# Opening the first feed-forward of a fused attention and SwiGLU kernel with interleaved groups, fillers in the first norm, and column-tiled sums of squares

## The chip, the cores and the metric

The kernel runs on one core of a Trainium2 chip. The metric is device time in microseconds (us); lower is better. A core has several engines that run side by side and meet at semaphores: TensorE (PE in the profile, with its weight loads as PEld), VectorE (DVE), ScalarE (ACT), GpSimd (POOL) and SyncE (SP), and DMA queues that move data between main memory and the on-chip memory. Matmuls write to PSUM, an accumulator memory of few buffers; ACT and DVE read it out.

## The reference

Eight batches of attention with a squared ReLU in place of the softmax, then a root-mean-square norm, then a SwiGLU feed-forward without biases:

```python
# q, k, v: (8 batches, 12 heads, 448 positions, 64)
scores = (1/8) * q @ k.T                       # per batch and head
attn   = maximum(scores, 0)**2 / 448
x      = attn @ v                              # to (3584 tokens, 768)
rms    = sqrt(mean(x*x, axis=-1) + 1e-6)
xn     = x / rms * rms_g
g      = xn @ w_gate                           # 768 -> 1536
out    = (g * sigmoid(g)) * (xn @ w_val) @ w_out   # 1536 -> 768
```

The norm stands between the two halves: no projection of a batch can start until all 768 features of the batch are known.

## The kernel before

One batch is 448 tokens, S. The features lie on the 128 partitions in 6 k tiles (KT), the 1536 hidden features in 12 blocks (FT). P is 128, D is 64. The program fixes the order on each engine itself: the feed-forward of batch b is the main list of units, the attention and the norm of batch b+1 are the side list, and `merge` lays the side units between the main ones by estimated cost. `head` and `tail` are the shares of the main list that stay free of side units at its start and at its end.

```python
def merge(main, side, head=0.0, tail=0.0):
    total = sum(c for c, _ in main)
    ...
    n = len(side)
    for c, f in main:
        while k < n and done >= total * (head + (1.0 - head - tail) * k / n):
            out.append(side[k][1])
            k += 1
        out.append(f)
        done += c
    out.extend(f for _, f in side[k:])
    return out
```

PSUM is shared out in three pools. All projections, output pieces, transposes, sums of squares and fillers take one of three buffers in turn:

```python
ps_s = ... tile_pool(name="ps_s", bufs=2, space=PSUM)   # scores
ps_a = ... tile_pool(name="ps_a", bufs=1, space=PSUM)   # attention times v
ps_m = ... tile_pool(name="ps_m", bufs=3, space=PSUM)   # all else
```

Fillers are matmuls on a tile of zeros whose result nobody reads:

```python
def keep_busy(n):
    ps = ps_m.tile([P, S], FP32, name="psB", tag="mm")
    for _ in range(n):
        nc.tensor.matmul(out=ps[:], lhsT=ones_bf[:], rhs=busy_bf[:], start=True, stop=True)
```

In the attention, a group of scores is four matmuls on the two row halves of the array, into both score buffers. ACT (or DVE) applies the ReLU out of PSUM, and the squares are put off to a later unit. `attend` multiplies by v, and the tile of the output and its square follow on ACT and DVE:

```python
def attend(b, j):
    psAV = ps_a.tile([P, S], FP32, name="psAV", tag="ps_a")
    ...                                    # 8 matmuls on column halves
    nc.scalar.mul(out=xT[:, j, :], in_=psAV[:], mul=inv_attn)
    pending.append(lambda: nc.vector.tensor_tensor(          # the square
        out=x2s[b][:, j, :], in0=xT[:, j, :], in1=xT[:, j, :], op=ALU.mult))
```

The norm sums the squares over the partitions with a matrix of ones, so that every partition gets the sum; ACT takes the root, DVE the reciprocal, and DVE scales the six tiles one after the other:

```python
def norm(b):
    psSS = ps_m.tile([P, S], FP32, name="psSS", tag="mm")
    for kt in range(KT):
        nc.tensor.matmul(out=psSS[:], lhsT=ones_bf[:], rhs=x2s[b][:, kt, :],
                         start=(kt == 0), stop=(kt == KT - 1))
    ...
    nc.scalar.activation(out=rstd[:], in_=psSS[:], func=ACT.Sqrt, ...)
    act_table(ACT.Silu)
    nc.vector.reciprocal(out=rstd[:], in_=rstd[:])
    for kt in range(KT):
        nc.vector.scalar_tensor_tensor(out=xn[:, kt, :], in0=xTs[b][:, kt, :],
            scalar=g_sb[:, kt : kt + 1], in1=rstd[:], op0=ALU.mult, op1=ALU.mult)
```

The feed-forward: for each of the 12 blocks a gate group and a value group of 12 matmuls (6 k tiles, two column halves of 64), each followed by its reader; then output pieces of 24 matmuls, 512 and 256 columns wide:

```python
def gate(b, fb):
    psG = project(wg_sb, b, fb, "psG")     # 12 matmuls on column halves
    nc.scalar.activation(out=s[:], in_=psG[:], func=ACT.Silu)
    ...
def value(b, fb):
    psV = project(wv_sb, b, fb, "psV")
    nc.vector.tensor_tensor(out=hTs[...][:, fb, o:o+S], in0=sil[b, fb][:], in1=psV[:], op=ALU.mult)

def ffn(b):
    for fb in range(FT):
        units.append((1.13, gate)); units.append((1.13, value))
    for t in ...:                          # 3 or 4 tiles of 128 tokens
        units.append((2.56, outproj 512)); units.append((1.28, outproj 256))
```

The whole runs as attention and norm of batch 0 alone, and then eight times a feed-forward merged with the next attention and norm:

```python
for fn in merge([], attention(0) + [(1.1, lambda: norm(0))]): fn()
...
for b in range(B):
    side = attention(b + 1) + [(1.1, norm(b + 1))]
    main = ffn(b)
    ...
    for fn in merge(main, side, 0.3 if b == 0 else 0.0, 0.15): fn()
```

Of the kernel before, what the change touches and what calls it, by code (L numbers as in the profile page):

```python
# [8 lines left out]
FP32 = mybir.dt.float32  # L9
# [8 lines left out]
def merge(main, side, head=0.0, tail=0.0):  # L18


    total = sum(c for c, _ in main)
    if not main:
        return [f for _, f in side]
    out, done, k = [], 0.0, 0
# [9 lines that stand above are left out]
# [3 lines left out]
def kernel(  # L37
# [11 lines left out]
    nc = tc.nc  # L49
    P = nc.NUM_PARTITIONS  # L50
    B, H, S, D = q.shape
    T, DM = out.shape
    _, F = moe_w_gate.shape
    assert (T, DM) == (B * S, H * D) and 2 * D == P and S % NCH == 0 and B % 2 == 0
    PC = S // NCH
    KT, FT, HP = DM // P, F // P, H // 2
# [19 lines left out]
    ps_m = ctx.enter_context(tc.tile_pool(name="ps_m", bufs=3, space=bass.MemoryType.PSUM))  # L76
# [8 lines left out]
    def load(nm, b, h0=0, h1=H):  # L85
        runs = nm == "v" or b < PE_T
        if (nm, b) not in ld:
            shape = [PC, H, NCH * D] if runs else [PC, NCH, H * D]
            ld[nm, b] = ldpool.tile(shape, BF16, name=nm + "b", tag=nm + "b")
        t = ld[nm, b]  # L90
        src = src_of[nm][b, h0:h1]
        if runs:
            nc.gpsimd.dma_start(out=t[:, h0:h1, :], in_=src.rearrange("h (p c) d -> p h (c d)", c=NCH))  # L93
        else:
            nc.gpsimd.dma_start(  # L95
                out=t[:].rearrange("p c (h d) -> p c h d", d=D)[:, :, h0:h1, :],
                in_=src.rearrange("h (p c) d -> p c h d", c=NCH),
            )
# [4 lines left out]
    def transpose_dma(b):  # L103
        new_qkT(b)
        for ti, nm in enumerate(("k", "q")):
            for c in range(NCH):
                nc.sync.dma_start_transpose(
                    out=qkT[b][:, :, ti, c * PC : (c + 1) * PC], in_=ld[nm, b][:, c, :]
                )

    wg_sb = wpool.tile([P, KT, F], BF16, name="wg_sb", tag="wg")
    wv_sb = wpool.tile([P, KT, F], BF16, name="wv_sb", tag="wv")
# [18 lines left out]
    ones_bf = const.tile([P, P], BF16, name="ones_bf", tag="ones_bf")  # L131
# [4 lines left out]
# [4 lines that stand above are left out]
# [9 lines left out]
    def act_table(func):  # L149
        nc.scalar.activation(out=scrap[:], in_=eps_col[:], func=func)  # L150
# [73 lines left out]
    x2s = {}  # L224
# [23 lines left out]
    def attention(b):  # L248
        units = []

        def add(cost, *fns):
            units.append((cost, lambda: [f() for f in fns]))

        if b < PE_T:
            add(0.4, lambda: transposes(b, 0))
        for j in range(HP):
            add(0.5, lambda j=j: scores(b, j, (0, 1)))
            if b < PE_T and j + 1 < HP:
                add(0.4, lambda j=j: transposes(b, j + 1))
            if b == 0:  # L260
                add(0.3, lambda: keep_busy(2))
            add(1.2, lambda j=j: scores(b, j, (2, 3)), lambda j=j: j and attend(b, j - 1))
            if b == 0:
                add(0.3, lambda: keep_busy(2))
        add(0.1, flush)
        add(0.8, lambda: attend(b, HP - 1), flush)
        return units


    xns, hTs = {}, {}  # L270

    def norm(b):
        psSS = ps_m.tile([P, S], FP32, name="psSS", tag="mm")
        for kt in range(KT):
            nc.tensor.matmul(  # L275
                out=psSS[:], lhsT=ones_bf[:], rhs=x2s[b][:, kt, :],
                start=(kt == 0), stop=(kt == KT - 1),
            )
        rstd = npool.tile([P, S], FP32, name="rstd", tag="rstd", bufs=1)
        nc.scalar.activation(  # L280
            out=rstd[:], in_=psSS[:], func=ACT.Sqrt, scale=1.0 / float(DM), bias=eps_col[:]
        )
        act_table(ACT.Silu)
        nc.vector.reciprocal(out=rstd[:], in_=rstd[:])  # L284
        xn = npool.tile([P, KT, S], BF16, name="xn", tag="xn")
        for kt in range(KT):
            nc.vector.scalar_tensor_tensor(  # L287
                out=xn[:, kt, :], in0=xTs[b][:, kt, :], scalar=g_sb[:, kt : kt + 1], in1=rstd[:],
                op0=ALU.mult, op1=ALU.mult,
            )  # L290
        xns[b] = xn
        if b % 2 == 0:
            hTs[b // 2] = hpool.tile([P, FT, 2 * S], BF16, name="hT", tag="hT")

    def project(w_sb, b, fb, nm):
        ps = ps_m.tile([P, S], FP32, name=nm, tag="mm")
        for kt in range(KT):
            for h in range(0, P, D):
                nc.tensor.matmul(  # L299
                    out=ps[h : h + D, :], lhsT=w_sb[:, kt, fb * P + h : fb * P + h + D],  # L300
                    rhs=xns[b][:, kt, :], start=(kt == 0), stop=(kt == KT - 1),
                )
        return ps

    sil = {}

    def gate(b, fb):
        psG = project(wg_sb, b, fb, "psG")
        s = spool.tile([P, S], BF16, name="sil", tag="sil")
        nc.scalar.activation(out=s[:], in_=psG[:], func=ACT.Silu)  # L310
        sil[b, fb] = s

    def value(b, fb):
        psV = project(wv_sb, b, fb, "psV")
        o = (b % 2) * S
        nc.vector.tensor_tensor(  # L316
            out=hTs[b // 2][:, fb, o : o + S], in0=sil[b, fb][:], in1=psV[:], op=ALU.mult
        )

    osts = {}  # L320

    def outproj(i, t, o, w):
        ps = ps_m.tile([P, 512], FP32, name="psO", tag="mm")
        for fk in range(FT):
            for h in range(0, P, D):
                nc.tensor.matmul(  # L326
                    out=ps[h : h + D, :w], lhsT=hTs[i][:, fk, t * P + h : t * P + h + D],
                    rhs=wo_sb[:, fk, o : o + w], start=(fk == 0), stop=(fk == FT - 1),
                )
        if o == 0:  # L330
            osts[i, t] = opool.tile([P, DM], FP32, name="ost", tag="ost")
        ost = osts[i, t]
        nc.scalar.copy(out=ost[:, o : o + w], in_=ps[:, :w])  # L333
        if o + w == DM:
            g, end = t * P, (t + 1) * P
            while g < end:
                n = min(end, (g // PC + 1) * PC) - g
                b, c, p0 = 2 * i + g // S, g % S // PC, g % PC
                rows = out[b * S : (b + 1) * S, :].rearrange("(p u) m -> p u m", u=NCH)
                nc.sync.dma_start(  # L340
                    out=rows[p0 : p0 + n, c, :], in_=ost[g - t * P : g - t * P + n, :]
                )
                g += n

    def ffn(b):
        units = []
        for fb in range(FT):
            units.append((1.13, lambda fb=fb: gate(b, fb)))
            units.append((1.13, lambda fb=fb: value(b, fb)))
        full = S // P  # L350
        for t in range(full) if b % 2 == 0 else range(full, NT):
            units.append((2.56, lambda t=t: outproj(b // 2, t, 0, 512)))
            units.append((1.28, lambda t=t: outproj(b // 2, t, 512, DM - 512)))
        return units

    keep_busy(16)
    for fn in merge([], attention(0) + [(1.1, lambda: norm(0))]):
        fn()
    for nm in ("q", "k", "v"):
        load(nm, 1)  # L360
    load_wo(0, 2)
    load_wo(1, 2)
    for b in range(B):
        side = []
        if b + 1 < B:
            side = attention(b + 1) + [(1.1, lambda b=b: norm(b + 1))]
        main = ffn(b)
        if b + 2 < B:
            for nm in ("q", "k", "v"):
                load(nm, b + 2)  # L370
            at = len(main) * 2 // 3
            main[at:at] = [(0, lambda b=b: transpose_dma(b + 2))]
        for fn in merge(main, side, 0.3 if b == 0 else 0.0, 0.15):
            fn()


# [28 lines left out]
```

## Time and profile before

| what | value |
|---|---|
| time, median of 3 runs | 475.36 us (475.14 to 478.07) |
| span of the profiled run | 473.7 us |
| TensorE clock granted, mean over the span | 0.991 of full speed |
| PE busy | 455.2 us, 4696 matmuls |
| DVE busy | 283.5 us |
| ACT busy | 254.1 us |
| GpSimd busy | 55.7 us |
| sums of squares (psSS) | 48 matmuls of 128 x 128 by 448, 8 norms |
| reciprocal in each norm | 2953 ns on DVE |
| one scaling of a tile (xn) | 681 ns on DVE, 48 of them |

The names in the profile are those of the program: psG and psV are the gate and value groups, psO the output pieces, psS the scores, psAV the attention times v, psT the transposes, psSS the sums of squares, psB the fillers. "128\*64" behind a matmul is the part of the array that it uses, rows by columns: 128\*128 is the whole, 128\*64 one column half, 64\*128 one row half. L299 is a line of the kernel. A matmul's length in the timeline runs from its start to the end of its pipeline, and matmuls overlap, so what a group costs is read from the start of one group to the start of the next.

### The profile page before, as it was taken

Reading aid. Unit: us, or ns where it says so; the run is one execution under the profiler, and the core shown is the slowest. Engines: PE = TensorE matmul, PEld = TensorE weight load, DVE = VectorE, ACT = ScalarE, POOL = GpSimd, SP = SyncE. Lnnn points to the kernel's source line nnn. Section 1 sums busy time; section 2 is a strip of 40 time slices with the busy share of each in tenths; the row PEclk is TensorE's granted clock in tenths of the full one; section 3 lists DMA queues with packets and bytes.
Section 4 is the critical chain, followed back from the end, with each engine's and each line's share of the span. In section 5 each row is a group of like instructions: output and inputs, shape, how many; then the busy total and the mean of one; then the engine's idle time right before and its main releaser. Section 6 shows DMA issues by size and latency. Waiting matters only on the chain.

```text
span 473.7 us, 10771 instructions
## 1 busy us (share of the span) xinstructions
PE 455.2 (96%) x4696; PEld 246.7 (52%) x4696; DVE 283.5 (60%) x449; ACT 254.1 (54%) x380; POOL 55.7 (12%) x48
## 2 busy tenths in 40 slices
PE   7877999899999999999999999999999999999995
PEld 2323654454556544564546554564546644566563
DVE  2875389467773676567673767657663776752210
ACT  3871366466555566556564566465654566452221
POOL 8463000430004000130004000000000000000000
PEclk9997999999999999999999999999999999999999
DMA  9999999999906990099204990077002200021013
GB/s 105 198 204 199 208 165 137 98 210 148 84 2 95 211 122 1 2 189 176 29 1 69 218 142 1 1 142 135 1 1 61 76 1 1 1 68 35 1 35 100
DMA packets 128046, 43.55 MB, mean 92 GB/s; under 512 B 100608, under 2 KB 124416, under 8 KB 128000
## 3 DMA queue, kind: packets, MB, share of 16 engines
q0 software_dynamic: 88944, 23.60, 51.5%
q1 hardware_dynamic: 39056, 19.28, 21.3%
q8 instruction: 36, 0.59, 0.5%
q14 instruction: 10, 0.08, 0.1%
HBM read 47.19 MB, written 11.01 MB: 123 GB/s over the span
## 4 chain that ended last, share of the span: by engine, by line
PE 89%; DVE 5%; ACT 2%; DMA 1%; issue 1%; POOL 0%; DVEq 0%; ACTq 0%; POOLq 0%
PE psG L299 24%; PE psV L299 24%; PE psO L326 22%; PE psS L201 9%; PE psAV L230 8%; PE psSS L275 2%; DVE r L218 2%; DVE rstd L284 1%; ACT r L215 1%; DMA kb<-in_k_dram 1%; DVE xn L287 1%; DVE r L213 1%; PE psT L174 1%; PE psB L139 0%; ACT rstd L280 0%
## 5 line engine op out<-in xcount | busy, mean ns | idle before, releaser
L215 ACT ACTIVATE r<-psS 112x896 bf16<-112x896 f32 x147 | 128.5, 915 | 49.9 <-PE psS L201 49.7
L299 PE MATMUL psG<-xn,wg_sb 128*64 128x448 bf16 x1152 | 129.5, 357 | 5.1 <-DVE xn L287 5.1
L299 PE MATMUL psV<-xn,wv_sb 128*64 128x448 bf16 x1152 | 126.7, 355 | 0.0
L316 DVE TENSOR_TENSOR hT<-sil,psV 128x448 bf16<-128x448 bf16 x96 | 59.6, 621 | 98.8 <-PE psV L299 97.8
L326 PE MATMUL psO<-wo_sb,hT 128*64 128x512 bf16 (+1 forms) x1344 | 113.2, 326 | 0.0
L218 DVE TENSOR_TENSOR r<-r 112x896 bf16<-112x896 bf16 x189 | 109.7, 626 | 0.2 <-ACT r L215 0.2
L310 ACT ACTIVATE sil<-psG 128x448 bf16<-128x448 f32 x96 | 52.3, 544 | 82.2 <-PE psG L299 82.2
L299 PEld LDWEIGHTS <-wg_sb 128*64 128x64 bf16 x1152 | 63.8, 110 | 58.5 <-issue 20.9
L326 PEld LDWEIGHTS <-hT 128*64 128x64 bf16 x1344 | 74.6, 110 | 37.5 <-issue 2.6
L299 PEld LDWEIGHTS <-wv_sb 128*64 128x64 bf16 x1152 | 65.3, 110 | 45.6 <-issue 5.2
L333 ACT COPY ost<-psO 128x512 f32<-128x512 f32 (+1 forms) x56 | 26.8, 479 | 71.1 <-PE psO L326 70.4
L213 DVE TENSOR_SCALAR r<-psS 112x896 bf16<-112x896 f32 x45 | 48.9, 1087 | 16.5 <-PE psS L201 16.5
L201 PE MATMUL psS<-qkT 64*128 64x448 bf16 x384 | 54.4, 354 | 4.6 <-ACT r L215 3.7
L230 PE MATMUL psAV<-r,vb 112*64 112x448 bf16 x384 | 46.1, 358 | 1.0 <-DVE r L218 1.0
L284 DVE RECIPROCAL rstd<-rstd 128x448 f32<-128x448 f32 x8 | 23.6, 2953 | 21.5 <-ACT rstd L280 21.5
L201 PEld LDWEIGHTS <-qkT 64*128 64x128 bf16 x384 | 12.1, 94 | 39.7 <-issue 35.7
L243 DVE TENSOR_TENSOR x<-xT 128x448 bf16<-128x448 bf16 x48 | 18.5, 385 | 22.2 <-ACT xT L241 22.2
L241 ACT ACTIVATE xT<-psAV 128x448 bf16<-128x448 f32 x48 | 26.1, 544 | 9.8 <-PE psAV L230 6.5
L230 PEld LDWEIGHTS <-vb 112*64 112x64 bf16 x384 | 18.4, 109 | 24.7 <-issue 15.3
L93 POOL DMA_DIRECT2D vb<-in_v_dram x9 | 8.3, 920 | 187.1 <-PE psAV L230 185.9
L287 DVE SCALAR_TENSOR_TENSOR xn<-xT,g_sb,rstd 128x448 bf16<-128x448 bf16 x48 | 29.3, 681 | 0.3
L95 POOL DMA_DIRECT2D qb<-in_q_dram x6 | 13.8, 2298 | 43.3 <-DMA qkT<-qb 37.2
(29 smaller groups left out, 116.0 us busy)
## 6 DMA issues: line engine op xcount, KB each, us to landing
qb<-in_q_dram POOLq DMA_DIRECT2D x7, 672.0 KB, 14.2
kb<-in_k_dram POOLq DMA_DIRECT2D x7, 672.0 KB, 22.5
vb<-in_v_dram POOLq DMA_DIRECT2D x7, 672.0 KB, 10.1
out_dram<-ost SPq DMA_DIRECT2D x8, 336.0 KB, 5.9
wg_sb<-in_moe_w_gate_dram POOLq DMA_DIRECT2D x4, 576.0 KB, 18.5
wv_sb<-in_moe_w_val_dram POOLq DMA_DIRECT2D x4, 576.0 KB, 20.1
wo_sb<-in_moe_w_out_dram POOLq DMA_DIRECT2D x2, 1152.0 KB, 26.1
out_dram<-ost SPq DMA_DIRECT2D x8, 288.0 KB, 5.1
```

Source lines behind the costliest of these rows:

```text
L201: nc.tensor.matmul(out=psS[:, hh, :S], lhsT=qkT[b][prt, j].rearrange("p t s -> p (t s)")[:, c * PC : c * PC + P], rhs=qkT[b][prt, j, 1, :] ...
L213: nc.vector.tensor_relu(out=r[:], in_=psS[:PC, :, :S])
L215: nc.scalar.activation(out=r[:], in_=psS[:PC, :, :S], func=ACT.Relu)
L218: lambda r=r, eng=eng: eng.tensor_tensor(out=r[:], in0=r[:], in1=r[:], op=ALU.mult)
L230: nc.tensor.matmul(out=psAV[hh * D : (hh + 1) * D, :], lhsT=ld["v", b][:, 2 * j + hh, c * D : (c + 1) * D], rhs=rsq[b, j, c][:, hh, :], st ...
L284: nc.vector.reciprocal(out=rstd[:], in_=rstd[:])
L287: nc.vector.scalar_tensor_tensor(out=xn[:, kt, :], in0=xTs[b][:, kt, :], scalar=g_sb[:, kt : kt + 1], in1=rstd[:], op0=ALU.mult, op1=ALU.mult,
L299: nc.tensor.matmul(out=ps[h : h + D, :], lhsT=w_sb[:, kt, fb * P + h : fb * P + h + D], rhs=xns[b][:, kt, :], start=(kt == 0), stop=(kt == ...
L310: nc.scalar.activation(out=s[:], in_=psG[:], func=ACT.Silu)
L316: nc.vector.tensor_tensor(out=hTs[b // 2][:, fb, o : o + S], in0=sil[b, fb][:], in1=psV[:], op=ALU.mult)
L326: nc.tensor.matmul(out=ps[h : h + D, :w], lhsT=hTs[i][:, fk, t * P + h : t * P + h + D], rhs=wo_sb[:, fk, o : o + w], start=(fk == 0), sto ...
L333: nc.scalar.copy(out=ost[:, o : o + w], in_=ps[:, :w])
```

## The change

Four edits. The sums of squares are made as the other projections are, by two column halves of 64 in place of one matmul of 128 columns, so that the array stays in the same mode as the work around them. Behind the first norm 24 fillers are put on TensorE, which otherwise has nothing to do until the scaled input arrives. The first feed-forward opens with three groups (gate 0, value 0, gate 1) that share the loop over k tiles, so that each scaled tile feeds three groups when it arrives. And `tail` goes from 0.15 to 0.18, so that attention and norm of the next batch are laid into the first 82 percent of the feed-forward.

```diff
     def norm(b):
         psSS = ps_m.tile([P, S], FP32, name="psSS", tag="mm")
         for kt in range(KT):
-            nc.tensor.matmul(
-                out=psSS[:], lhsT=ones_bf[:], rhs=x2s[b][:, kt, :],
-                start=(kt == 0), stop=(kt == KT - 1),
-            )
+            for h in range(0, P, D):
+                nc.tensor.matmul(
+                    out=psSS[h : h + D, :], lhsT=ones_bf[:, h : h + D], rhs=x2s[b][:, kt, :],
+                    start=(kt == 0), stop=(kt == KT - 1),
+                )
 ...
-    def project(w_sb, b, fb, nm):
-        ps = ps_m.tile([P, S], FP32, name=nm, tag="mm")
+    def project(b, *groups):
+        pss = [ps_m.tile([P, S], FP32, name="psP", tag="mm") for _ in groups]
         for kt in range(KT):
-            for h in range(0, P, D):
-                nc.tensor.matmul(
-                    out=ps[h : h + D, :], lhsT=w_sb[:, kt, fb * P + h : fb * P + h + D],
-                    rhs=xns[b][:, kt, :], start=(kt == 0), stop=(kt == KT - 1),
-                )
-        return ps
+            for ps, (w_sb, fb) in zip(pss, groups):
+                for h in range(0, P, D):
+                    nc.tensor.matmul(
+                        out=ps[h : h + D, :], lhsT=w_sb[:, kt, fb * P + h : fb * P + h + D],
+                        rhs=xns[b][:, kt, :], start=(kt == 0), stop=(kt == KT - 1),
+                    )
+        return pss
 ...                       # gate and value as before, split into matmuls and reader
+    def gate_value_gate(b):
+        g0, v0, g1 = project(b, (wg_sb, 0), (wv_sb, 0), (wg_sb, 1))
+        silu(b, 0, g0)
+        hidden(b, 0, v0)
+        silu(b, 1, g1)
 ...
     def ffn(b):
         units = []
+        if b == 0:
+            units.append((3.4, lambda: gate_value_gate(b)))
         for fb in range(FT):
-            units.append((1.13, lambda fb=fb: gate(b, fb)))
-            units.append((1.13, lambda fb=fb: value(b, fb)))
+            if b or fb > 1:
+                units.append((1.13, lambda fb=fb: gate(b, fb)))
+            if b or fb:
+                units.append((1.13, lambda fb=fb: value(b, fb)))
 ...
     for fn in merge([], attention(0) + [(1.1, lambda: norm(0))]):
         fn()
+    keep_busy(24)
 ...
-        for fn in merge(main, side, 0.3 if b == 0 else 0.0, 0.15):
+        for fn in merge(main, side, 0.3 if b == 0 else 0.0, 0.18):
             fn()
```

In the profile after, gate and value groups share the name psP.

## The prediction

> **What bounds the kernel now.** I read the page first (busy shares, the clock row), then the chain of waits, then the list of who waited for whom, and last the timeline of the few stretches where TensorE is not simply streaming.
>
> ```profile
> PE 455.2 (96%) x4696; PEld 246.7 (52%) x4696; DVE 283.5 (60%) x449; ACT 254.1 (54%) x380; POOL 55.7 (12%) x48
> PEclk9997999999999999999999999999999999999999
> PE 89%; DVE 5%; ACT 2%; DMA 1%; issue 1%; POOL 0%; DVEq 0%; ACTq 0%; POOLq 0%
> ```
>
> TensorE is the bound, 96% busy and 89% of the chain. The clock row has one dip, the fourth slice (35.5 to 47.4 us). Only two kinds of wait of a matmul on other engines are of note:
>
> ```profile
> PE psG L299 <- DVE xn L287: 5.1, 4, 4.4
> PE psS L201 <- ACT r L215: 3.7, 8, 1.0
> ```
>
> The first norm, in the timeline (start, length, instruction group, in brackets the idle time before it):
>
> ```profile
> 33.05 1.47 PE L275 MATMUL psSS<-x,ones_bf 128*128 128x448 bf16 x6
> 34.56 0.63 ACT L280 ACTIVATE rstd<-psSS,eps_col 128x448 f32<-128x448 f32 x1 [0.86 <-PE psSS L275]
> 35.22 2.95 DVE L284 RECIPROCAL rstd<-rstd 128x448 f32<-128x448 f32 x1 [1.11 <-ACT rstd L280]
> 38.95 3.56 PE L299 MATMUL psG<-xn,wg_sb 128*64 128x448 bf16 x12 [4.43 <-DVE xn L287]
> 42.25 2.50 PE L299 MATMUL psV<-xn,wv_sb 128*64 128x448 bf16 x12
> 44.49 1.92 PE L299 MATMUL psG<-xn,wg_sb 128*64 128x448 bf16 x12
> 46.22 1.32 PE L299 MATMUL psV<-xn,wv_sb 128*64 128x448 bf16 x12
> ```
>
> A matmul row's length includes its pipeline, so I count start to start. A group of 12 takes 1.135 us in steady state (46.22, 47.35, 48.49 in the same timeline: 94.5 ns an instruction, 189 ns a pair on the two column halves). Here the first gate group takes 3.30 us, the next two 2.24 and 1.73. Windows of one microsecond tell why; the column before the DMA share is the clock:
>
> ```profile
> 42.00:43.00 1.00, 1.00 (x6) 0.57 (x7) 0.00 (x0) 0.45 (x1) 0.00 (x0) 0.50 1.46 198
> 45.00:46.00 1.00, 1.00 (x10) 0.64 (x8) 0.48 (x1) 0.00 (x0) 0.68 (x1) 0.66 1.46 199
> 46.00:47.00 1.00, 1.00 (x15) 0.71 (x11) 0.00 (x0) 0.54 (x1) 1.00 (x1) 1.00 1.45 196
> ```
>
> Half clock from 39 us to about 45.5 us. The second place is the end of the second attention, laid into the first feed-forward:
>
> ```profile
> 84.54 0.55 PE L201 MATMUL psS<-qkT 64*128 64x448 bf16 x4
> 86.10 0.36 PE L201 MATMUL psS<-qkT 64*128 64x448 bf16 x2 [1.01 <-ACT r L215]
> 86.91 0.36 PE L201 MATMUL psS<-qkT 64*128 64x448 bf16 x2 [0.44 <-ACT r L215]
> 87.21 0.95 PE L230 MATMUL psAV<-r,vb 112*64 112x448 bf16 x8
> ...
> 100.56 0.92 PE L299 MATMUL psG<-xn,wg_sb 128*64 128x448 bf16 x6
> ...
> 103.07 1.33 PE L299 MATMUL psV<-xn,wv_sb 128*64 128x448 bf16 x12
> ```
>
> Two score groups stand back to back, and the second waits for the two score buffers to be emptied. Later the second norm's scaled input comes too late for the next gate group (2.51 us, 100.56 to 103.07). From 104 to 426 us the waits list has no wait of a matmul on another engine. The third norm shows what a sum of squares costs there:
>
> ```profile
> 146.90 1.48 PE L326 MATMUL psO<-wo_sb,hT 128*64 128x256 bf16 x24
> 148.31 1.31 PE L275 MATMUL psSS<-x,ones_bf 128*128 128x448 bf16 x6
> 149.55 7.99 PE L326 MATMUL psO<-wo_sb,hT 128*64 128x512 bf16 x96
> ```
>
> **What the Trainium skill says.** "TensorE: Matmul & The Clock Gate", Part 1: after about one idle window of 3.4 us the TensorE clock falls to one half, and sustained activity of about such a window is needed to bring it back. The trace agrees on the fall (4.43 us idle, then 0.50); the return took about 6 us of thin and then dense work. "TensorEngine Tiling (Array Packing)", Key Properties: changing the tiling mode drains the array. The trace agrees: a score group of 4 (64-row tiles) between two projections, from 56.95 to 57.44 us, costs 0.49 for two pairs that would stream in 0.38, and the group ahead of it 1.26 in place of 1.135, so about 0.11 to 0.12 us for each change. "TensorE: Matmul & The Clock Gate", Part 3, The mechanism: matmuls start and end in program order. So one matmul that waits holds everything behind it, which matters for the rival below.
>
> **The change part by part.**
>
> First norm and first feed-forward. The end of the sum of squares is set by the last squared tile (DVE, 33.73 to 34.12 us), not by the matmuls, so column tiling gains nothing here and the scaled tiles xn appear when they do now: the pairs of the gate start at 38.95, 39.55, 40.14, 40.74, 41.34, 41.93, one per 0.6 us. The 24 fillers take 24 x 0.189 = 4.54 us; from 34.34 with one mode change 0.11 they end at 39.0, almost exactly when xn arrives (they cost perhaps 0.15 us there), and the clock stays full. Three groups by k tile need 6 x 94.5 = 0.57 us for each tile, against 0.6 us of supply: the last tile is done at 41.94 + 0.57 = 42.5. The next group, value 1, needs a fourth buffer of a pool of three, so it waits for the first gate to be read: its last pair starts at 41.94, the activation can start 0.42 later (as at full clock elsewhere: second-next group at 47.35, activation of the one before at 48.72, last pair at 48.30), takes 0.54, so 42.95. Before, this same group began at 46.22. Gain 3.27 us. Weights are no hindrance: the first slices of both were issued at 7.7 and 8.5 us, and the slowest took 22.8 us to land.
>
> Rest of that feed-forward. From 46.22 to 103.07 before is 56.85 us. Pure streaming in that stretch: 22 projection groups x 1.135 = 25.0; three output tiles x 3.9 = 11.7; 13 score groups x 0.608 with their two mode changes = 7.9; six attends x 0.77 = 4.6; six transposes x 0.4 = 2.4; sum of squares 1.24; together 52.8. (The two joined score groups save 0.23 of it.) The difference, 4.2 us, is waiting: 84.54 to 87.21 is 2.67 in place of 0.87 (1.8); the last attend 89.30 to 90.79 is 1.49 in place of 0.78 (0.7); the gate 2.51 in place of 1.14 (1.4); a score group at 77.02 with 0.78 in place of 0.49 (0.3). In the built order of the changed program the last two score groups have an output tile (2.6 us) between them, and the norm is followed by four output pieces (7.8 us) in place of three (5.2). Scaled input is complete 8.0 us after the sum of squares (94.8 to 102.8), so with 7.8 + 0.5 of other work ahead of the gate nothing is left to wait for. All four waits go, 4.2 us; one more pair of mode changes costs 0.23; sum of squares column-tiled saves 0.2 (two changes of mode; its 12 half matmuls stream in 6 x 0.189, as the 6 full ones did); but it now stands directly behind the last attend. A last squared tile comes 1.39 us after that attend's last pair starts (first norm: 32.73 to 34.12), the first five pairs cover 0.19 + 0.945 = 1.135, so 0.28 us of waiting is new. Net 4.2 - 0.23 + 0.2 - 0.28 = 3.9; I take off 0.2 for small waits where a transpose now stands between score groups in place of a projection: 3.7.
>
> The six later norms. In the three with an odd number the order keeps an output piece between last attend and sum of squares: 0.2 each, 0.6. In the three with an even number it stands directly behind: 0.2 - 0.28, -0.24 together. Gain 0.36. Moving the norm earlier by 1.3 us buys nothing more here, as nothing waited.
>
> Sum: 3.3 + 3.7 + 0.4 = 7.4 us, 475.36 - 7.4 = 468.0.
>
> **Rivals.** (a) The fillers do harm: 24 are too many, or zeros do not hold the clock. For it: they end within 0.1 us of the arrival of xn. Against: the zero-fed fillers in the first attention go with a clock of 1.00 up to 34 us. If the clock fell anyway, interleaving alone would still fill the tile waits, but at half clock three groups take 18 x 0.38 = 6.8 us: 39 to 45.8, a gain of under 1 us in this part, and 470.5 in all. (b) DMA becomes the bound in the first feed-forward: the queues are full there (tenths at 9 through slice ten), and everything on TensorE comes up to 7 us sooner. Keys of batch 1 were issued at 32.06 and landed 16.4 later, at 48.5, needed at about 52; the output weights landed by 63.5, needed at about 78; the transposed batch 2 is complete near 87, needed at about 93. All have slack, so I give this little; it would take back 1 to 4 us: 469 to 472. (c) The attend to norm adjacency bites in four places and harder than 0.28 us, because ACT is in order and loads a table (1.28 us) nearby. The load stands behind the copy of the last attend, so it delays the root, which has slack, not the squares. If each costs 0.6: +1.3, 469.3. (d) The waits of 4.2 us partly reappear elsewhere, since ACT and DVE have the same work in a shorter stretch: half of them back is 470. In favour of more: nothing found; all waiting of the stretch is already in the sum.
>
> **Range and chances.** The two parts of 3.3 and 3.7 us are each fixed by several rows and bounded above by the waits that exist, about 8.5 us of all that I found. So the low side is short, the high side longer: 466.0 to 470.8. Faster by over 2% needs 465.85, more than I find in the profile: 0.07. Slower by 2% would need a new stall of 17 us: 0.02.
>
> **What would show it.** The clock row without its dip; windows of 39 to 46 us at 1.00; the second value group (the first with 12 in a row after the interleaved ones) starting near 43 us; the gate of batch 1 following without a pause, the value behind it near 96 us in place of 103.07; sums of squares next to output pieces taking 1.14; a wait of about 0.3 us before the last pair where an attend stands ahead. Wrong would be: a clock of 0.5 behind the fillers, a value 1 group well past 43.5, new waits of score groups on ACT, or matmuls that wait on DMA between 43 and 96 us.

## The result and the profile after

The changed kernel takes 468.43 us (468.10 to 468.78) beside 475.25 us (474.70 to 478.07) of the kernel before on the same chip: ratio 0.9845, 95% interval 0.9805 to 0.9885. It is faster by about 6.8 us, clear of noise and within 2 percent. The prediction was 468.0.

The page, the busy line and the clock row:

```profile
PE 454.5 (97%) x4768; PEld 257.6 (55%) x4768; DVE 283.6 (61%) x449; ACT 252.5 (54%) x380; POOL 55.8 (12%) x48
PEclk9999999999999999999999999999999999999999
```

TensorE's busy time hardly changes (it has 24 fillers and 48 half matmuls more, and no half-clock stretch); the dip of the clock row is gone. What changed is read in the timeline, start to start. The first norm and the opening (start, length, instructions, idle time before; most of the interleaved rows and those of other engines are left out):

```profile
32.40 1.63 PE L276 MATMUL psSS<-x,ones_bf 128*64 128x448 bf16 x12
33.97 4.71 PE L139 MATMUL psB<-busy_bf,ones_bf 128*128 128x448 bf16 x24
38.61 0.38 PE L302 MATMUL psP<-xn,wg_sb 128*64 128x448 bf16 x2
...
41.85 0.36 PE L302 MATMUL psP<-xn,wg_sb 128*64 128x448 bf16 x2
41.87 0.98 ACT L312 ACTIVATE sil<-psP 128x448 bf16<-128x448 f32 x2 [5.65 <-PE psP L302]
42.46 1.33 PE L302 MATMUL psP<-xn,wv_sb 128*64 128x448 bf16 x12 [0.26 <-ACT sil L312]
43.60 1.33 PE L302 MATMUL psP<-xn,wg_sb 128*64 128x448 bf16 x12
```

The fillers run from 33.97 to 38.6 us. The three groups take 3.4 us, from 38.61 to the end of the pair that starts at 41.85 (0.19 us); one group alone took 3.3 before. Then the fourth group, value 1, waits for the activation to empty a buffer, and from there each group takes 1.14 us. One window of that stretch (the column before the DMA share is the clock):

```profile
39.00:41.00 2.00, 2.00 (x24) 1.46 (x22) 2.00 (x5) 0.00 (x0) 0.00 (x0) 1.00 1.44 199
```

The end of the attention of batch 1, laid into this feed-forward:

```profile
81.08 0.55 PE L201 MATMUL psS<-qkT 64*128 64x448 bf16 x4
81.56 0.95 PE L230 MATMUL psAV<-r,vb 112*64 112x448 bf16 x8
...
81.67 1.09 DVE L213 TENSOR_SCALAR r<-psS 112x896 bf16<-112x896 f32 x1 [1.59 <-PE psS L201]
...
82.68 2.22 DVE L218 TENSOR_TENSOR r<-r 112x896 bf16<-112x896 bf16 x4
83.65 0.61 PE L230 MATMUL psAV<-r,vb 112*64 112x448 bf16 x4
84.42 0.38 PE L230 MATMUL psAV<-r,vb 112*64 112x448 bf16 x2 [0.15 <-DVE r L218]
84.96 0.38 PE L230 MATMUL psAV<-r,vb 112*64 112x448 bf16 x2 [0.16 <-DVE r L218]
85.15 1.63 PE L276 MATMUL psSS<-x,ones_bf 128*64 128x448 bf16 x12
86.58 7.99 PE L339 MATMUL psO<-wo_sb,hT 128*64 128x512 bf16 x96
...
94.99 1.33 PE L302 MATMUL psP<-xn,wg_sb 128*64 128x448 bf16 x12
96.15 1.30 PE L302 MATMUL psP<-xn,wv_sb 128*64 128x448 bf16 x12
```

The score group passes without its wait (0.48 us; before, 2.67 us for two joined groups) and the gate at 94.99 takes 1.16 in place of 2.51. But the last attend, from 83.65 to 85.15, still takes 1.50 us for 0.76 us of work (8 matmuls of 94.5 ns): it waits for the squares of its scores, which come late from DVE. Before, it took 1.49 us:

```profile
89.30 0.61 PE L230 MATMUL psAV<-r,vb 112*64 112x448 bf16 x4
...
90.60 0.38 PE L230 MATMUL psAV<-r,vb 112*64 112x448 bf16 x2 [0.15 <-DVE r L218]
90.79 2.78 PE L326 MATMUL psO<-wo_sb,hT 128*64 128x512 bf16 x24
```

And the sum of squares behind it takes 1.43 where its matmuls alone stream in 1.14.

Two later norms, of batches 2 and 3:

```profile
139.96 1.30 PE L276 MATMUL psSS<-x,ones_bf 128*64 128x448 bf16 x12
141.09 9.28 PE L339 MATMUL psO<-wo_sb,hT 128*64 128x256 bf16 x120
...
191.85 1.61 PE L276 MATMUL psSS<-x,ones_bf 128*64 128x448 bf16 x12
193.27 9.30 PE L339 MATMUL psO<-wo_sb,hT 128*64 128x256 bf16 x120
```

Batch 2 has an output piece ahead of its sum of squares: 1.13 us. Batch 3 has an attend ahead of it: 1.42, so 0.29 of waiting.

The first attention, which no edit touches, ends at other times in other executions (its last pair of matmuls at 32.15 to 34.26 us in the twelve profiles). So I compare three stretches in each profile: from that pair to value 1 of batch 0 (A), from there to value 0 of batch 1 (B), from there to the end of the span (C). All in us, read from the timelines, one execution for each kernel. A and B are good to about 0.02 us; C to about 0.1, as the span is given to a tenth. The median times were taken in several sets, in which the kernel before had medians of 474.78 to 475.27 us, so a gain of under a microsecond is read from the stretches and not from the times.

| kernel | time, median | A | B | C |
|---|---|---|---|---|
| before | 475.25 | 13.49 | 56.85 | 370.63 |
| changed | 468.43 | 10.24 | 53.69 | 370.15 |
| e1 fillers and interleaving only | 472.08 | 10.21 | 56.84 | 370.75 |
| e2 82 percent only | 472.30 | 13.28 | 53.77 | 371.20 |
| e3 column tiling only | 473.16 | 12.86 | 56.84 | 369.35 |
| e4 changed, no fillers | 470.48 | 11.72 | 53.69 | 370.25 |
| e5 changed, no interleaving | 469.93 | 11.69 | 53.69 | 370.26 |
| e6 changed, 82 percent in the first only | 467.64 | 10.25 | 53.68 | 369.27 |
| e7 changed, squares earlier | 467.59 | 10.25 | 52.93 | 370.25 |
| e8 e6, e7 and another buffer | 465.98 | 9.82 | 52.90 | 369.28 |
| e9 e8 with 20 fillers | 466.24 | 9.79 | 52.94 | 369.28 |
| e10 changed, 8 fillers | 468.67 | 11.75 | 53.69 | 370.21 |

Between before and changed, A gives 3.25, B 3.16, C 0.48: 6.9 us, beside 6.8 between the median times. In the three kernels that keep the old opening, A itself differs: 13.49 (before), 13.28 (E2) and 12.86 (E3), because the half-clock stretch starts at another moment in each (see the last section). With another execution of the kernel before, the gain of A could thus have read 2.6. The span of the profiles differs by 7.4 because the first attention happened to end 0.5 us sooner.

### The profile page after: what moved, and what is told of

It is laid out like the page before. It is cut to its first block, busy times and chain, and to the rows that moved or that the text cites. A ratio compares the mean times of both kernels' runs of the same rounds, so it can differ in the third digit from the quotient of the medians.

```text
span 466.3 us, 10899 instructions
## 1 busy us (share of the span) xinstructions
PE 454.5 (97%) x4768; PEld 257.6 (55%) x4768; DVE 283.6 (61%) x449; ACT 252.5 (54%) x380; POOL 55.8 (12%) x48
## 4 chain that ended last, share of the span: by engine, by line
PE 91%; DVE 3%; ACT 2%; DMA 1%; issue 1%; POOL 0%; ACTq 0%; DVEq 0%; POOLq 0%
PE psP L302 48%; PE psO L339 23%; PE psS L201 9%; PE psAV L230 8%; DVE r L218 2%; PE psB L139 1%; PE psSS L276 1%; DMA kb<-in_k_dram 1%; ACT r L215 1%; DVE r L213 1%; PE psT L174 1%; ACT xT L241 1%; DVE x L243 0%; POOL qb L93 0%; POOL kb L93 0%
## 5 line engine op out<-in xcount | busy, mean ns | idle before, releaser
L302 PE MATMUL psP<-xn,wv_sb 128*64 128x448 bf16 x1152 | 126.9, 353 | 0.3 <-ACT sil L312 0.3
L302 PE MATMUL psP<-xn,wg_sb 128*64 128x448 bf16 x1152 | 126.8, 353 | 0.0
L317 DVE TENSOR_TENSOR hT<-sil,psP 128x448 bf16<-128x448 bf16 x96 | 59.6, 621 | 84.7 <-PE psP L302 82.6
L312 ACT ACTIVATE sil<-psP 128x448 bf16<-128x448 f32 x96 | 52.2, 545 | 97.2 <-PE psP L302 97.1
L339 PEld LDWEIGHTS <-hT 128*64 128x64 bf16 x1344 | 78.9, 110 | 31.7 <-issue 0.4
L302 PEld LDWEIGHTS <-wg_sb 128*64 128x64 bf16 x1152 | 66.4, 110 | 45.4 <-issue 7.4
```

The lines of the kernel that those rows point to most:

```text
L302: nc.tensor.matmul(out=ps[h : h + D, :], lhsT=w_sb[:, kt, fb * P + h : fb * P + h + D], rhs=xns[b][:, kt, :], start=(kt == 0), stop=(kt == ...
L317: nc.vector.tensor_tensor(out=hTs[b // 2][:, fb, o : o + S], in0=sil[b, fb][:], in1=psV[:], op=ALU.mult)
L339: nc.tensor.matmul(out=ps[h : h + D, :w], lhsT=hTs[i][:, fk, t * P + h : t * P + h + D], rhs=wo_sb[:, fk, o : o + w], start=(fk == 0), sto ...
```

## The experiments

**E1: fillers and interleaving alone.** The changed kernel with the sum of squares and the share put back:

```diff
-            for h in range(0, P, D):
-                nc.tensor.matmul(out=psSS[h : h + D, :], lhsT=ones_bf[:, h : h + D], ...)
+            nc.tensor.matmul(out=psSS[:], lhsT=ones_bf[:], ...)
...
-        for fn in merge(main, side, 0.3 if b == 0 else 0.0, 0.18):
+        for fn in merge(main, side, 0.3 if b == 0 else 0.0, 0.15):
```

> Fillers and interleaved opening only; sums of squares whole and the norm at 85 percent, as before. My ledger: all of the first part and nothing else, 3.2 us, so 472.0 us; value 1 starts near 42.5 us, the stretch from there to value 0 of batch 1 still takes about 56.8 us with its score waits and its late norm. Rival (the gain of the later stretch is a consequence of the warm and early start, not of the order): 469 us or less, and the stretch is near 53.7 us as in the changed kernel.

Measured 472.08 us, ratio 0.9937 (0.9910 to 0.9963). A is 10.21, as in the changed kernel; B is 56.84, as before to 0.01 us. So the first part is worth 3.3 us, needs no column tiling, and the later stretch gains nothing from a warm and early start. The rival falls.

**E2: 82 percent alone.** The kernel before with one number changed:

```diff
-        for fn in merge(main, side, 0.3 if b == 0 else 0.0, 0.15):
+        for fn in merge(main, side, 0.3 if b == 0 else 0.0, 0.18):
```

> Only the share of 82 percent. My ledger: the joined score groups (1.8), the late gate (1.4) and one short score wait (0.3) go, one pair of mode changes comes (0.23), and four sums of squares now wait for their last tile (about 0.2 each with whole matmuls): net 2.5 us, so 472.8 us. The wait of the last attend (0.7) stays. Rival (packing the attention more densely gives the waits back elsewhere): 474 to 476 us, with new waits of scores on ACT.

Measured 472.30 us, ratio 0.9932 (0.9907 to 0.9956). B falls by 3.08 us to 53.77 and C grows by 0.57: the order alone makes the gain of B, and it costs in the later norms, where three sums of squares now wait. The time fell by 3.0 rather than the 2.5 expected; 0.2 of that is A, in which this execution's half-clock stretch began, and so ended, sooner. The rival's new waits of scores on ACT are not there: 2.3 us in the list of waits of the whole span, 3.7 before, and none between 43 and 104 us, where before had 1.5.

**E3: column tiling alone.** The kernel before with the sum of squares of the change.

> Only the column-tiled sums of squares. With the norm at 85 percent every one of the seven later norms stands between output pieces, so two mode changes go in each: 7 x 0.2 = 1.4 us, 473.9 us; a sum of squares takes 1.14 us start to start and the piece ahead of it loses its 0.10. Rival (twice the instructions cost time of their own, or the change of mode is not what the 0.2 us is): 475.2 us or more.

Measured 473.16 us, ratio 0.9960 (0.9945 to 0.9976), so 1.1 to 2.6 us; the expected 1.4 lies inside, but it is made up otherwise. C falls by 1.28 for six norms, 0.21 each. The third norm:

```profile
146.18 1.48 PE L327 MATMUL psO<-wo_sb,hT 128*64 128x256 bf16 x24
147.49 1.30 PE L276 MATMUL psSS<-x,ones_bf 128*64 128x448 bf16 x12
148.62 7.97 PE L327 MATMUL psO<-wo_sb,hT 128*64 128x512 bf16 x96
```

From output piece to output piece it takes 2.44 us where it took 2.65 before; the piece ahead loses 0.10 and the sum of squares 0.11, and its 12 half matmuls take the 1.13 that 6 whole ones would. The seventh norm, in B, brings nothing (56.84 beside 56.85): the gate behind it waits for its scaled tiles anyway. A is 0.6 shorter, but not through the tiling, which leaves the norm's end alone: from the last attend's pair to the first gate it is 6.25 us here and 6.22 before. The half-clock stretch came sooner in this execution, and the group from 44.37 already took 1.14.

**E4: no fillers.**

```diff
-    keep_busy(24)
```

> The changed kernel without its 24 fillers. If the clock falls in the pause and comes back after some 3.4 to 6 us of dense work: three groups at half clock until about 43.5 us, value 1 near 44.8 us in place of 42.5, 470.8 us (469.5 to 471.7). Rival (interleaving alone does it, because the supply of scaled tiles is the limit and half clock does not matter): value 1 by 43, 468.5 us.

Measured 470.48 us, ratio 0.9894 (0.9867 to 0.9921). Windows of its trace (the column behind PE busy is the clock):

```profile
40.00:41.00 1.00, 1.00 (x8) 0.50 1.43 196
41.00:42.00 1.00, 1.00 (x9) 0.54 1.47 200
42.00:43.00 1.00, 1.00 (x14) 1.00 1.46 198
```

Half clock, 8 or 9 matmul starts in a microsecond, until just short of 42 us. A is 11.72, 1.48 more than with fillers; B and C are unchanged. The mechanism is the expected one, but in this execution the clock came back 1.6 us earlier than I took it to, so the loss in A is 1.5 and not 2.3. The profiled execution, 469.87 us, is the fastest of six. Three of the six have a mean clock of 0.993 and took 469.87 to 470.30; the other three have 0.991 and took 470.66 to 470.77, which is the loss of 2.3 us that I had expected. That their half clock lasted longer fits the lower mean, but no trace shows it.

**E5: no interleaving.** Fillers stay; gate 0, value 0 and gate 1 come one after the other.

```diff
     def ffn(b):
         units = []
-        if b == 0:
-            units.append((3.4, lambda: gate_value_gate(b)))
         for fb in range(FT):
-            if b or fb > 1:
+            if True:
                 units.append((1.13, lambda fb=fb: gate(b, fb)))
-            if b or fb:
+            if True:
                 units.append((1.13, lambda fb=fb: value(b, fb)))
```

> The changed kernel with fillers but with gate 0, value 0, gate 1 one after the other. Clock stays full; gate 0 is paced by the scaled tiles to about 41.65 us, two groups of 1.135 follow, value 1 at about 43.9 in place of 42.5: 1.45 us lost, 469.9 us. Rival (the clock was everything and the order of the groups does not matter): 468.5 us.

Measured 469.93 us, ratio 0.9902 (0.9884 to 0.9920). A is 11.69: 1.45 lost, as expected. Against the 13.49 of before, interleaving alone (E4) gets 1.77 and fillers alone (E5) 1.80; together they are worth 3.25, so about 0.3 us is counted in both. The profile is of the slowest of the six executions, 471.68 us: its first attention ended 2 us later than that of the changed kernel, which none of the three stretches contains.

**E6: 82 percent only in the first feed-forward.**

```diff
-        for fn in merge(main, side, 0.3 if b == 0 else 0.0, 0.18):
+        for fn in merge(main, side, 0.3 if b == 0 else 0.0, 0.18 if b == 0 else 0.15):
```

> 82 percent only in the first feed-forward, 85 percent in the later ones. My ledger: the sums of squares of batches 3, 5 and 7 again have an output piece ahead of them, so three waits of 0.28 us go: 0.85 us faster than the changed kernel, 467.6 us, and the gates behind the norms still do not wait. Rival (the earlier norm is needed there too): gates wait for scaled tiles and the time is 468.5 us or more.

Measured 467.64 us, ratio to before 0.9843 (0.9825 to 0.9860). The norm of batch 3 in its timeline:

```profile
192.53 1.48 PE L339 MATMUL psO<-wo_sb,hT 128*64 128x256 bf16 x24
193.84 1.30 PE L276 MATMUL psSS<-x,ones_bf 128*64 128x448 bf16 x12
194.97 7.97 PE L339 MATMUL psO<-wo_sb,hT 128*64 128x512 bf16 x96
```

The output piece is back ahead of the sum of squares, which takes 1.13; C falls by 0.88, three waits of 0.29. No gate waits for scaled tiles. In the later feed-forwards the earlier norm cost and brought nothing.

**E7: squares earlier.** In `scores`, the squares of the group before are issued ahead of the ReLU in one place:

```diff
+        if (b, j, cs) == (1, HP - 1, (2, 3)):
+            flush()
         squares = []
         for c, psS in zip(cs, pss):
             ...                          # ReLU of this group
         flush()                          # squares of the group before
```

> The changed kernel with the squares of the last batch-1 scores 0 and 1 issued on DVE ahead of the ReLU of score 3 in place of behind it. If the wait of the last attend in the first feed-forward (1.50 us for 0.78 us of work) is DVE's queue order, it takes 0.8 us and the whole is 0.7 us faster: 467.7 us. Rival (the wait is the length of the chain scores, ReLU, square, however ordered): no change, 468.4 us, or the wait moves to the sum of squares behind it.

Measured 467.59 us, ratio to before 0.9849 (0.9831 to 0.9867). The same place as above, in its timeline:

```profile
81.06 1.15 DVE L220 TENSOR_TENSOR r<-r 112x896 bf16<-112x896 bf16 x2
...
82.73 1.09 DVE L215 TENSOR_SCALAR r<-psS 112x896 bf16<-112x896 f32 x1 [0.52 <-PE psS L201]
...
83.73 1.15 DVE L220 TENSOR_TENSOR r<-r 112x896 bf16<-112x896 bf16 x2
84.71 0.93 PE L232 MATMUL psAV<-r,vb 112*64 112x448 bf16 x8
85.47 1.61 PE L278 MATMUL psSS<-x,ones_bf 128*64 128x448 bf16 x12
```

DVE now does two of the four squares while it used to sit idle ahead of the ReLU, only two are left behind it, and the attend runs through in 0.76. B falls by 0.76. It was DVE's queue order; the rival falls. The sum of squares behind it still waits.

**E8: E6, E7 and another buffer.** The third of the interleaved groups goes to the pool of the attention, which is empty at that time:

```diff
-        pss = [ps_m.tile([P, S], FP32, name="psP", tag="mm") for _ in groups]
+        pss = [ps_m.tile(..., tag="mm") if i < 2 else ps_a.tile(..., tag="ps_a")
+               for i in range(len(groups))]
```

> E6 and e7 together, and the third of the interleaved groups in the buffer of the attention (free at that time), so that value 1 need not wait for the first activation (0.45 us between the end of the three groups and value 1). 0.85 + 0.7 + 0.45 = 2.0 us faster than the changed kernel: 466.4 us. If the parts hide one another, 467 to 468.

Measured 465.98 us, ratio to before 0.9825 (0.9801 to 0.9848). It beats both kernels. A falls by 0.42 (value 1 no longer waits for a buffer), B by 0.79, C by 0.87: together 2.08 of the 2.0 expected, so the parts do not hide one another. The medians differ by 2.4, but they come from different sets. One of its five executions took 468.93 us at a mean clock of 0.990; where its clock fell is not known.

**E9: 20 fillers in E8.**

```diff
-    keep_busy(24)
+    keep_busy(20)
```

> E8 with 20 fillers in place of 24, so that the last filler ends 0.7 us before the first scaled tile arrives. In the changed kernel the first interleaved matmul starts 0.14 us later behind the fillers than it does without them. If that is the fillers' overhang, the span from the last attend to value 1 shrinks from 9.82 to 9.68 us and the whole by 0.14 us, within the noise of the times. Rival (a pause of under a microsecond costs clock): it grows.

Measured 466.24 us, ratio to before 0.9819 (0.9795 to 0.9842); A is 9.79, 0.03 less, a miss. The pause of 0.63 us does not cost clock. The first interleaved matmul starts 0.83 us after DVE begins to scale the first tile; it is 0.88 with 24 fillers (changed, E8) and 0.74 without any (E4). So only 0.05 of the 0.14 us is the fillers' overhang. The other 0.09 stays with 20 fillers and, in E10, even behind a pause of 2.9 us; what it is, no run settles. The overhang is worth only 0.03 us in A because the end of the three groups is set by the arrival of the last scaled tiles: the rows that hold the first matmuls of tiles 5 and 6 start at 40.91 and 41.50, 0.59 apart, where 0.57 would stream.

**E10: 8 fillers in the changed kernel.**

```diff
-    keep_busy(24)
+    keep_busy(8)
```

> The changed kernel with 8 fillers in place of 24: TensorE is busy to about 35.5 us and idle for 2.9 us, where without fillers it is idle for 4.4. If the clock falls only after an idle stretch of the length of a window (3.4 us by the skill's page on the matmul and the clock gate), it holds here and value 1 comes 10.1 us after the last attend, time 468.3 us. If a pause of about 3 us is enough, it is as without fillers: 11.7 us, 470.4 us.

Measured 468.67 us, ratio to before 0.9871 (0.9849 to 0.9893). Neither expectation holds for all executions: two of six had a mean clock of 0.993 and took 469.60 and 469.71 us, four had 0.998 to 1.0 and took 468.47 to 468.73. The profiled one is of the first kind: 2.90 us idle, half clock from about 38.3 to 41.7 us, A 11.75, as long as with no fillers at all. For the other of the two the place of the fall is inferred from its time and mean clock; E5's profile has the same mean, and its clock fell in the first attention. After the full 4.43 us of pause, in e4, all six executions had 0.991 to 0.993.

## Why the prediction was right, point by point

**First norm and opening, 3.27 us predicted.** A gives 3.25, and E1 alone gives all of it. The supply of tiles, the length of the three groups and the wait of value 1 for the activation were each as worked out: the fourth group starts 10.24 us after the last attend's pair; by the prediction's numbers it was 42.95 - 32.73 = 10.22. (Its terms, 41.94 + 0.42 + 0.54, add to 42.90; the trace has the missing 0.05 us between the end of the activation and value 1.) That column tiling gains nothing here holds (E1). The 0.15 us for the fillers is seen at the first matmul (0.14), but hardly reaches value 1 (E9). The agreement to 0.02 us is in part luck: both sides use the same execution of the kernel before, whose A is the longest of the three.

**Rest of that feed-forward, 3.7 us predicted.** B gives 3.16, and E2 shows that the order makes 3.08 of it. Three of the four waits went, as said: the joined score groups, the late gate, the short score wait. The step that failed is "All four waits go": the wait of the last attend (0.7) stayed whole, 1.50 us for 0.76 of work. The prediction counted on the output tile between the last two score groups, and did not follow the squares. In the program's DVE queue two of the four squares that this attend needs stand behind the ReLU of the next score group, and so all four come at the end. E7 moves the two ahead, and 0.76 us goes. The 0.2 us taken off for other small waits covered a part of the miss, by luck: between 43 and 97 us the list of waits of matmuls has the last attend alone, and 3.9 - 0.74 is the 3.16 measured. The new wait between attend and sum of squares was put at 0.28 and is 0.29 to 0.30.

**Later norms, 0.36 us predicted.** C gives 0.48. The parts are shown one by one: column tiling 0.21 a norm (E3), an attend ahead of the sum of squares 0.29 of waiting (E6); six times the one less three times the other is 0.4. That moving the norm earlier there buys nothing is shown by E6, where moving it back gains 0.88.

**The rivals.** Of (a), the fillers hold the clock. Its size for a fallen clock, a gain of under 1 us in A, was too gloomy for the profiled execution of E4, which still gains 1.8 there, as its clock is back by 42 us; for the three with a mean clock of 0.991 it is not known. Of (b), DMA, nothing is to be seen: no matmul waits on DMA between 43 and 97 us, and B is the same to 0.01 us in E4 and E5, which start it 1.5 us later. Of (c), the adjacency costs 0.3 and not 0.6. Of (d), one wait did stay, but in its old place and not as a new one.

## What to carry to other kernels

Where one engine is busy 96 percent, the rest is a ledger of single waits: read each from start to start in the timeline against the streaming time of the same group, and the sum forecasts the gain: here 7.4 us against 6.9 in the stretches, with one wait misjudged. Before counting a wait as gone, follow the whole chain into the in-order queue of the other engine: here the producer had time, but its queue held the wrong instruction first. And a knob that is right in one stage (the norm at 82 percent in the first feed-forward) should be set for that stage alone; in the others it moved a sum of squares up against its own producer.

## What the hardware showed that I had not expected

The half clock came in one length or its double. In windows of 0.25 us it lasted 6.83 us in before, E2 and E3, and 3.42 us in E4, E10 and, inside the first attention, E5. What varied was when it began: 6.1, 5.7 and 4.8 us after the start of the last attend's pair in before, E2 and E3, whose A is 13.49, 13.28 and 12.86. So an earlier fall cost less work, and an apparent early return in E3 is an early fall. The two profiles with one length at this place, E4 and E10, have the interleaved opening; whether denser work is the reason, or only the moment, no run settles.

The fall is not a fixed function of the pause. After the first norm 2.9 us idle brought the clock down in E10's profile, 4.4 us in those of before, E2, E3 and E4, and 0.6 us not in E9's. In the first attention, behind the same short work, 1.16 us was enough in E5's, and 1.65 us was not in E7's. The Trainium skill ("TensorE: Matmul & The Clock Gate", Part 1) calls the activity window, of about 3.4 us, free-running, which agrees with stretches of 3.42 and 6.83 us that begin at different moments. That the clock falls after one idle window of that length, as the prediction has it from the same part, is not borne out: pauses of 2.9 and 1.16 us were enough.

A change between whole matmuls and column halves costs 0.10 to 0.11 us each way (E3: 0.21 for the pair). The run shows the cost, not what it consists of.
